# Reordering the SyncE queue of each chunk in an mLSTM cell followed by a squared-ReLU FFN

## Chip, cores, metric

The kernel runs on one core of a Trainium2 chip. The time is device microseconds of that core, the median of five runs. TensorE is called PE below, VectorE DVE, ScalarE ACT, GpSimd POOL, and SyncE SP; SP does no arithmetic here, it issues nearly all DMAs.

## The reference

Two stages. First an mLSTM cell for 4 batches x 8 heads, 768 steps, head size 40:

```python
m_new = np.maximum(f_gate[:, :, t] + m, i_gate[:, :, t])
f_stab = np.exp(f_gate[:, :, t] + m - m_new)
i_stab = np.exp(i_gate[:, :, t] - m_new)
C = f_stab * C + i_stab * outer(vt, kt);  n = f_stab * n + i_stab * kt
y[:, :, t] = sigmoid(o_gate) * (C @ qt) / max(abs(n @ qt), 1)
```

Then the heads of a step are laid side by side into x, 3072 tokens x 320, and an FFN follows:

```python
h = np.maximum(x @ w_in, 0.0)        # 320 -> 2048
return h * h @ w_out                 # 2048 -> 320
```

## The kernel before

**Tiling.** A chunk s is 128 steps of one batch with all eight heads: 24 chunks, six per batch. Inside a chunk the recurrence becomes masked attention: scores k·q, a decay matrix W made from the gates, values, and a state C that is carried from chunk to chunk. Two chunks make one FFN group g of 256 tokens; there are 12 groups. Both FFN products run as Strassen-like block products, which need sums of x (`sums_of_x`, on POOL), of the hidden layer (`sums`, L760, on DVE) and of the weights.

**The interleaving.** The order of every engine's instructions is written by hand. The main loop (`for n, (which, g, i) in enumerate(parts)`) works on chunk s = 6 + n//4, in four parts `at` = 0 to 3. From s = 8 on, an even chunk runs beside the second FFN product (`ffn2_fast`, PE line L765) and an odd one beside the first (`ffn1_open` and `ffn1_close`, PE lines L841 and L890; `fast` is true there). One even and one odd chunk make a period; attention ends with s = 23 and the FFN goes on alone.

**The round trips through DRAM.** Three things are turned around by writing rows to a DRAM buffer and reading them back in another order:

- `pair_up(s + 3)` (L305): four DRAM-to-DRAM copies of k and q of a later chunk. `load_squares(s + 2)` (L327) reads them back in four DMAs as 32 x 32 squares, and DVE turns those (`turn_kq`, L334).
- `store_num` (L580) writes the attention's numerator tn; `load_num` (L585) brings it back in four DMAs; DVE then normalises it into x_sb (`normalise_turned`, first instruction L597, last L606).
- `store_rows` (L632) writes x_sb; `load_rows` (L637) reads it back as squares in four DMAs into xT; DVE turns those (`turn_squares`, L644). `sums_of_x` and the first FFN product of the group then read xT.

**What else SP issues for a chunk.** `load_part(s + 4, 0)` and `(…, 2)` (L945) for k and v; `load_A(s + 2)` (L352), the gate sums; `load_o(s + 4)` (L342), the output gates; and the FFN's result rows (L801 and L806 in even chunks). SP works this list strictly in order: an instruction that waits holds up all behind it. The output gates get their sigmoid four chunks at a time, in part 3 of chunks 11, 15 and 19 (`sigmoid`, L345 on ACT); the last of the four is the chunk s + 4 that was asked for in part 1 of the same chunk.

**What stands behind those on DVE and ACT.** On DVE, in an even chunk: `turn_kq` (L334), `weighted` (L467), `ffn2_fast`'s first add (L781), tn (L568), `turn_squares` of the odd chunk before (L644), then `sums` (S4, L760), an add (L781), `scale_q` (L515), and further adds. On ACT after the sigmoid: the ReLU L907 and the copy L785, which PE's L765 of the next chunk needs. PE holds its PSUM banks until DVE's L908 to L911 have read them.

Of the kernel before, what the change touches and what calls it, by code (L numbers as in the profile page):

```python
# [29 lines left out]
def kernel(  # L30
# [259 lines left out]
    def load_parts(s):  # L290
        d = st.setdefault(s, {})
        kq, va = d["kq"], d["va"] = kq_b[s % NKQ], va_b[s % NKQ]
        return (kq[:, 0, :, :D], k), (kq[:, 1, :, :D], q), (va[:, :, :D], v)
# [4 lines left out]
    KQ_SQ, X_SQ = 7, 6  # L298
# [37 lines left out]
    def load_o(s):  # L336
        b, c = divmod(s, NB)
        r, (s0, s1) = next((r, (a, z)) for r, (a, z) in enumerate(RUNS) if a <= s < z)
        if s == s0:
            st["og", r] = ld.tile([P, 4, H, D], F32, name="og")  # L340
        og = st.setdefault(s, {})["og"] = st["og", r][:, s - s0]
        nc.sync.dma_start(og, o_gate[b, :, c * P : (c + 1) * P, :].rearrange("h p d -> p h d"))  # L342

    def sigmoid(s):
        nc.scalar.activation(st[s]["og"], st[s]["og"], AF.Sigmoid)  # L345
# [89 lines left out]
    def scores(s, o=(False, False)):  # L435
        d = st[s]

        sc = [bank(o[i]) for i in range(2)]
        d["sc"] = sc
        if s >= KQ_SQ:  # L440
            for j in range(PR):
                for keys in HALVES:
                    for i in range(2):
                        rows = slice(DP * i, DP * i + D)
                        nc.tensor.matmul(
                            sc[i][keys, j, :], lhsT=d["kT"][rows, j, keys], rhs=d["qT"][rows, j, :], start=(j == 0),
                            stop=True, skip_group_check=True,
                        )
            return
        for j in range(PR):  # L450
            for i in range(2):
                rows = slice(DP * i, DP * i + D)
                nc.tensor.matmul(
                    sc[i][:, j, :], lhsT=d["kT"][rows, j, :], rhs=d["qT"][rows, j, :], start=True, stop=True,
                )
# [279 lines left out]
    def sums_of_weights(i):  # L735
        if i < 3:
            T[i] = late.tile([P, NPAIR, DH], F32, name=f"T{i}", bufs=1)[:]
        if i == 0:
            nc.vector.tensor_tensor(T[0], B12, B11, op=ALU.subtract)
        elif i == 1:  # L740
            nc.vector.tensor_tensor(T[1], B22, T[0], op=ALU.subtract)
        elif i == 2:
            nc.vector.tensor_tensor(T[2], B21, T[1], op=ALU.subtract)
        else:

            nc.vector.tensor_tensor(B12, B22, B12, op=ALU.subtract)
# [99 lines left out]
    def ffn1_begin(g):  # L846
        new_g2(g)
        xT = st["xT", g]
        begun = st["begun"] = [
            (ps_h.tile([P, 4, P], F32, name="h_ps"), ffn.tile([P, 4, P], F32, name="r_sb", bufs=4)) for _ in range(2)  # L850
        ]
        for q, (X, m1) in enumerate(begun):
            blocks(X, F11, xT[:, 0, 0, :], q, True)
            nc.scalar.copy(m1[:], X[:])
        for q, (X, m1) in enumerate(begun):
            blocks(X, F12, xT[:, 0, 1, :], q, False)
# [21 lines left out]
    def ffn1_rows(g, q, first):  # L878
        xT, xs = st["xT", g], st["xs"]
        X, Y, V, Z = st["f1"]  # L880
        lo, hi = HALVES
        pairs = (
            ((X, lo, xT[lo, 0, 2, :], False), (Y, hi, xT[hi, 1, 2, :], first)),
            ((V, lo, xT[lo, 1, 2, :], first), (Z, hi, xs[hi, 1, :], False)),
        )
        for pair in pairs:
            for n in range(4):
                for cols in HALVES:
                    for to, rows, rhs, start in pair:
                        nc.tensor.matmul(  # L890
                            to[cols, n, :], lhsT=w_in2[rows, 4 * q + n, cols], rhs=rhs,
                            start=(start and n == 0), stop=True, skip_group_check=True,
                        )
# [29 lines left out]
    def do(f, s):  # L923
        if 0 <= s < NT:
            f(s)
# [16 lines left out]
    def load_part(s, i):  # L942
        b, c = divmod(s, NB)
        dst, src = load_parts(s)[i]
        nc.sync.dma_start(dst, src[b, :, c * P : (c + 1) * P, :].rearrange("h p d -> p h d"))  # L945
# [65 lines left out]
    for u in range(8):  # L1011
        s = 2 + u // 2
# [69 lines left out]
            parts += [(1, g + 2, i) for i in range(4)]  # L1082
    LAST = (17, 17, 18, 18, 18)
    assert LAST[-1] == len(pieces)
    for n, (which, g, i) in enumerate(parts):
        s, at = 6 + n // 4, n % 4
        if n == 5:
            brought.close()
            late = ctx.enter_context(tc.tile_pool(name="late", bufs=1, side="right"))
        even = s >= 8 and s % 2 == 0  # L1090
        fast = which == 1
        if at == 0:
            if s < 8 or even:
                do(scores, s)
            if even:
                do(turn_kq, s + 1)
            if s < 8 or even:
                do(weighted, s)
        if at == 1:
            if even:  # L1100
                do(lambda s: scores(s, ("h", "h")), s + 1)
            if fast:
                ffn1_rows(g, 0, True)
            do(attend_turned, s)
            do(decays, s + 1)
            do(mask, s + 1)
            if n > 4 and not even and not fast:
                do(turn_kq, s + 1)
            do(decay_C, s + 1)
            if s > X_SQ and not fast:  # L1110
                do(turn_squares, s - 1)
            do(store_num, s)
            if s > 6:
                do(lambda s: load_part(s, 0), s + 4)
                do(load_num, s)
                if not even:
                    do(load_squares, s + 2)
                do(load_A, s + 2)
                do(lambda s: load_part(s, 2), s + 4)
                if 8 <= s < 20:  # L1120
                    load_o(s + 4)
            else:
                do(load, s + 4)
                do(load_num, s)
            do(pair_up, s + 3)
        if 5 <= n < 8:
            sums_of_weights(n - 5)
        if n == 6:
            sums(1, slice(0, NPAIR), (1, 2))
        if n == 8:  # L1130
            sums_of_weights(3)
            sums(1, slice(0, NPAIR), (3,))
        if n == 9:
            sums(1, slice(0, NPAIR), (4,))
        if which == 2 and i == 3 and g == NG - 2:
            sums(g + 1, slice(0, NPAIR), (2,))
        if which == 2 and g > 1 and i < 2:
            sums(g, slice(0, NPAIR), (3 + i,))
        if n == 0:
            ffn1_begin(g)  # L1140
            sums_of_x(g)
            sums_of_win(2)
        if at == 3 and s >= 8 and s % 2 == 0 and s // 2 - 1 < NG:
            sums_of_x(s // 2 - 1)
        if at == 2 and not fast:
            if n > 4:
                do(scale_q, s + 1)
        if at == 3:
            if s % 4 == 3:
                for r in range(s + 1, min(s + 5, NT)):  # L1150
                    sigmoid(r)
        if fast:
            if i % 2:
                ffn1_close(g, i // 2, i == 1)
                if at == 1 and g > 2:
                    do(turn_kq, s + 1)
                    do(turn_squares, s - 1)
            else:
                ffn1_open(g, i // 2)
                if i == 0 and g > 2:  # L1160
                    sums(g - 1, slice(0, NPAIR), (2,))
            if at == 2 and g > 2:
                do(scale_q, s + 1)
        elif g == 0:
            ffn2(g, *divmod(i, 2))
        else:
            ffn2_fast(g, i)
        if at == 2:
            do(lambda s: weigh(s, masked=True), s + 1)
            ffn1_square()  # L1170
            if n < 4:
                do(turn_kq, s + 1)
                do(scale_q, s + 1)
            if even:
                do(weighted, s + 1)
            do(normalise_turned, s)
            do(store_rows, s)
            if s < 7 or even:
                do(load_squares, s + 2)
            do(load_rows, s)  # L1180
            if s < 7:
                do(load_A, s + 2)
        if at == 0:
            ffn1_square()
        if n < 5:
            while rounding.done < LAST[n]:
                rounding.step()
# [30 lines left out]
```

## Time and profile before

| | us |
|---|---|
| median of 5 runs | 510.88 (507.30 to 512.22) |
| profiled execution, its own time | 508.48 |
| span of the profiled execution | 506.7 |
| PE busy | 493.7 (97%) |
| weight loads busy | 457.1 (90%) |
| DVE busy | 350.4 (69%) |
| ACT busy | 249.6 (49%) |

The profiled execution has 1.8 us around its span and lies 2.4 us under the median. The granted TensorE clock was 1.00. PE's busy share is made of overlapping matmuls whose ends are modelled, so it is read together with the time that a period takes.

### The profile page before, as it was taken

Reading aid. Unit: us, or ns where it says so; the run is one execution under the profiler, and the core shown is the slowest. Engines: PE = TensorE matmul, PEld = TensorE weight load, DVE = VectorE, ACT = ScalarE, POOL = GpSimd, SP = SyncE. Lnnn points to the kernel's source line nnn. Section 1 sums busy time; section 2 is a strip of 40 time slices with the busy share of each in tenths; the row PEclk is TensorE's granted clock in tenths of the full one; section 3 lists DMA queues with packets and bytes.
Section 4 is the critical chain, followed back from the end, with each engine's and each line's share of the span. In section 5 each row is a group of like instructions: output and inputs, shape, how many; then the busy total and the mean of one; then the engine's idle time right before and its main releaser. Section 6 shows DMA issues by size and latency. Waiting matters only on the chain.

```text
span 506.7 us, 13829 instructions
## 1 busy us (share of the span) xinstructions
PE 493.7 (97%) x5640; PEld 457.1 (90%) x5641; DVE 350.4 (69%) x646; ACT 249.6 (49%) x492; POOL 118.4 (23%) x138
## 2 busy tenths in 40 slices
PE   9988999999999999999999989999999999999997
PEld 4867878897799999999999988999989999999997
DVE  8588968889956956847937738757658866635441
ACT  3767888853541650672641752551753550433400
POOL 3346743321232031013033014024005030020000
PEclk9999999999999999999999999999999999999999
DMA  9999899856747747748847757667656632210000
GB/s 190 226 215 209 249 211 188 192 100 141 157 116 162 146 108 159 159 115 164 164 103 159 149 122 166 127 153 162 117 144 143 124 91 51 71 25 15 1 27 26
DMA packets 238238, 67.74 MB, mean 134 GB/s; under 512 B 185600, under 2 KB 232704, under 8 KB 238176
## 3 DMA queue, kind: packets, MB, share of 16 engines
q1 hardware_dynamic: 238080, 66.68, 61.7%
q8 instruction: 44, 0.72, 0.6%
q10 hardware_dynamic: 96, 0.20, 0.1%
q14 instruction: 18, 0.15, 0.1%
HBM read 54.56 MB, written 17.86 MB: 143 GB/s over the span
## 4 chain that ended last, share of the span: by engine, by line
PE 72%; SPq 8%; DMA 8%; DVE 4%; ACT 3%; issue 3%; POOL 1%; DVEq 0%; POOLq 0%; ACTq 0%
PE h_ps L765 23%; PE h_ps L841 19%; PE h_ps L890 6%; PE h_ps L674 4%; PE h_ps L711 3%; PE numT L551 3%; SPq L327 2%; DMA og<-in_o_gate_dram 2%; DMA num_rows<-tn 2%; DMA xT<-x_rows 2%; SPq L305 2%; PE hp L490 2%; SPq L585 2%; DMA x_rows<-x_sb 2%; PE idle L934 1%
## 5 line engine op out<-in xcount | busy, mean ns | idle before, releaser
L377 POOL TENSOR_SCALAR_AFFINE_SELECT A_bc<-A_bc 128x1024 f32<-128x1024 f32 x22 | 24.6, 1118 | 139.2 <-ACT kq L387 123.6
L765 PE MATMUL h_ps<-T,S 128*128 128x160 f32 x352 | 51.5, 299 | 0.8 <-DVE g_c L909 0.8
L765 PEld LDWEIGHTS h_ps<-T,S 128*128 128x128 f32 x352 | 49.0, 190 | 1.0 <-PE h_ps L765 1.0
L765 PE MATMUL h_ps<-w_out,g 128*128 128x160 f32 x336 | 49.2, 303 | 0.4 <-ACT y_sb L785 0.4
L765 PEld LDWEIGHTS h_ps<-w_out,g 128*128 128x128 f32 x336 | 46.1, 190 | 1.9 <-issue 1.2
L401 ACT ACTIVATE A_bc<-A_bc,b_T 128x128 f32<-128x128 f32 x144 | 44.2, 391 | 6.7 <-POOL A_bc L377 6.4
L871 ACT COPY r_sb<-h_ps 128x512 f32<-128x512 f32 x18 | 10.6, 587 | 72.2 <-PE h_ps L841 72.2
L841 PE MATMUL h_ps<-xT,w_in 128*128 128x128 f32 x320 | 42.8, 278 | 0.0
L841 PE MATMUL h_ps<-lent_t,w_in 128*128 128x128 f32 x320 | 42.2, 275 | 0.0
L841 PEld LDWEIGHTS h_ps<-xT,w_in 128*128 128x128 f32 x320 | 38.9, 192 | 1.0 <-issue 0.7
L890 PE MATMUL h_ps<-xT,w_in 64*64 64x128 f32 x960 | 39.7, 273 | 0.0
L841 PE MATMUL h_ps<-lent_t 128*128 128x128 f32 x320 | 39.2, 276 | 0.1
L841 PEld LDWEIGHTS h_ps<-lent_t,w_in 128*128 128x128 f32 x320 | 38.9, 192 | 0.0
L841 PEld LDWEIGHTS h_ps<-lent_t 128*128 128x128 f32 x320 | 37.3, 192 | 0.5 <-POOL lent_t L836 0.3
L890 PEld LDWEIGHTS h_ps<-xT,w_in 64*64 64x64 f32 x960 | 34.8, 133 | 2.5
L781 DVE TENSOR_TENSOR y_sb<-y_sb,h_ps 128x160 f32<-128x160 f32 x44 | 14.0, 318 | 29.9 <-PE h_ps L765 29.8
L413 POOL TENSOR_TENSOR vw<-va,A_bc 128x328 f32<-128x328 f32 x15 | 13.6, 904 | 78.4 <-issue 45.9
L674 PE MATMUL h_ps<-xT,w_in 128*128 128x256 f32 x128 | 29.6, 383 | 1.2 <-POOL w_in L230 0.6
L568 DVE STREAM_TRANSPOSE tn<-numT 128x256 f32<-128x256 f32 x36 | 15.6, 446 | 22.0 <-PE numT L551 22.0
L765 PE MATMUL h_ps<-w_out,g_c 128*128 128x160 f32 x192 | 28.0, 302 | 1.4 <-ACT y_sb L785 1.4
L644 DVE STREAM_TRANSPOSE xT<-xT 128x384 f32<-128x384 f32 x18 | 10.1, 559 | 26.4 <-DMA xT<-x_rows 26.4
L765 PEld LDWEIGHTS h_ps<-w_out,g_c 128*128 128x128 f32 x192 | 26.3, 190 | 2.1 <-ACT y_sb L785 1.5
(188 smaller groups left out, 1082.0 us busy)
## 6 DMA issues: line engine op xcount, KB each, us to landing
A_bc<-a_rows SPq DMA_DIRECT2D x22, 512.0 KB, 4.8
num_rows<-tn SPq DMA_DIRECT2D x18, 256.0 KB, 2.4
kq<-num_rows SPq DMA_DIRECT2D x72, 64.0 KB, 2.0
raw<-in_moe_w_out_dram SPq DMA_DIRECT2D x7, 640.0 KB, 4.2
kqT<-kq_rows SPq DMA_DIRECT2D x34, 128.0 KB, 3.4
kq<-in_k_dram SPq DMA_DIRECT2D x24, 160.0 KB, 4.0
va<-in_v_dram SPq DMA_DIRECT2D x24, 160.0 KB, 5.0
og<-in_o_gate_dram SPq DMA_DIRECT2D x24, 160.0 KB, 4.8
```

The costliest lines, as they stand in the source:

```text
L377: nc.gpsimd.affine_select(A[:], A[:], compare_op=ALU.is_ge, fill=-1e30, base=0, pattern=[[0, H], [1, P]], channel_multiplier=-1,)
L401: nc.scalar.activation(d["W"][:, i * n + h, :], A[i][:, h, :], AF.Exp, bias=b_T[:, b, c, i * n + h : i * n + h + 1],)
L413: nc.gpsimd.tensor_tensor(d["vw"][:], d["va"][:], d["W"][:, :, P - 1 : P].to_broadcast([P, H, D1]), op=ALU.mult,)
L551: nc.tensor.matmul(numT[i][halves[g], e, :], lhsT=va_w[s % NKQ][:, h * D1 : h * D1 + DP], rhs=d["P"][h % 2][:, h // 2, :] if s < KQ_SQ els ...
L568: nc.vector.transpose(to[:, 2 * i : 2 * i + 2], numT[i][:, :2, :].rearrange("p c t -> p (c t)"))
L674: nc.tensor.matmul(hs[i][:, n, :], lhsT=w_in[:, a, fb * P : (fb + 1) * P], rhs=xT[:, :, a, :], start=(n == 0 and a == 0), stop=False,)
L711: nc.tensor.matmul(o_ps, lhsT=st["g2", g][:, fb, j * P : (j + 1) * P], rhs=w_out[:, fb, :], start=(fb == 0), stop=(fb == NF - 1),)
L765: nc.tensor.matmul(to, lhsT=lhsT[:, p], rhs=rhs[:, p, :], start=(start and p == 0), stop=(p == NPAIR - 1), skip_group_check=True,)
L781: add = lambda to, a, b: nc.vector.tensor_tensor(to, a, b, op=ALU.add)
L841: nc.tensor.matmul(to[:, n, :], lhsT=lhsT[:, 4 * q + n, :], rhs=rhs, start=(start and n == 0), stop=True, skip_group_check=True,)
L871: nc.scalar.copy(m1[:], X[:])
L890: nc.tensor.matmul(to[cols, n, :], lhsT=w_in2[rows, 4 * q + n, cols], rhs=rhs, start=(start and n == 0), stop=True, skip_group_check=True,)
```

## The change

Only the order of SP's list changes, and the place of one DVE instruction. No instruction is added or removed: SP has the same DMAs before and after, and so have the others.

SP's list for a chunk from s = 8 on, waits left out:

| | before | after |
|---|---|---|
| even s | num store, k, num load x4, A, v, gates, copies x4, L801, x store, squares x4, x load x4, L806 | num store, k, num load x4, squares x4, A, L801, x store, v, gates, x load x4, copies x4, L806 |
| odd s | num store, k, num load x4, squares x4, A, v, gates, copies x4, x store, x load x4 | num store, k, num load x4, squares x4, x store, A, v, gates, x load x4, copies x4 |

Chunk 7 is changed like an odd one (it has no gates; an FFN row store goes ahead of the x store). On DVE, in even chunks, `turn_squares` of the odd chunk before moves from part 1 to part 2: it now comes after S4 and the first add behind it, and ahead of `scale_q`.

```diff
+    def prefetch(s):
+        do(lambda s: load_part(s, 2), s + 4)
+        if 8 <= s < 20:
+            load_o(s + 4)
...
-            if s > X_SQ and not fast:
+            if s > X_SQ and not fast and not even:
                 do(turn_squares, s - 1)
             do(store_num, s)
             if s > 6:
                 do(lambda s: load_part(s, 0), s + 4)
                 do(load_num, s)
-                if not even:
-                    do(load_squares, s + 2)
-                do(load_A, s + 2)
-                do(lambda s: load_part(s, 2), s + 4)
-                if 8 <= s < 20:
-                    load_o(s + 4)
+                do(load_squares, s + 2)
+                if even:
+                    do(load_A, s + 2)
             else:
                 do(load, s + 4)
                 do(load_num, s)
-            do(pair_up, s + 3)
+                do(pair_up, s + 3)
...
         if at == 2 and not fast:
+            if even:
+                do(turn_squares, s - 1)
             if n > 4:
                 do(scale_q, s + 1)
...
             do(store_rows, s)
-            if s < 7 or even:
+            if s < 7:
                 do(load_squares, s + 2)
+            else:
+                if not even:
+                    do(load_A, s + 2)
+                prefetch(s)
             do(load_rows, s)
-            if s < 7:
+            if s > 6:
+                do(pair_up, s + 3)
+            else:
                 do(load_A, s + 2)
```

## The prediction

> **What bounds the kernel.** I read the windows view first, one row per period (odd chunk, then even chunk), cut where PE starts the odd chunk's first L841. Columns: stretch, its length, busy time of each engine.
>
> ```profile
> 154.96:192.53 37.57, 37.57 (x514) 36.55 (x513) 27.35 (x55) 16.88 (x34) 8.43 (x10) 1.00 0.67 144
> 229.83:268.74 38.91, 38.16 (x515) 36.70 (x514) 27.51 (x55) 16.88 (x34) 10.57 (x14) 1.00 0.68 142
> 268.74:308.81 40.07, 37.85 (x514) 36.51 (x513) 26.68 (x54) 21.06 (x40) 8.24 (x9) 1.00 0.66 142
> 345.95:385.20 39.25, 38.16 (x515) 36.68 (x514) 26.25 (x50) 21.13 (x40) 6.86 (x8) 1.00 0.63 134
> ```
>
> A period with the same matmuls takes 37.57 when nothing stops PE. Three take 1.3, 2.5 and 1.7 more; with 0.4 and 0.2 in two others, all stalls from chunk 8 on are about 6 us. That is all a new order can win. The Trainium skill (Perfetto Trace Analysis, "Identifying the Most-Contended Engine") says to judge headroom by weight-load busy share, not matmul busy: here 90%, so 10%, or 50 us. The stall-free row has weight loads at 36.55 of 37.57, so what a period can give back is the 6 us; I take the rows.
>
> Next, PE's rows in order of time, with the idle time ahead of each and its releaser:
>
> ```profile
> 218.86 1.35 PE L765 MATMUL h_ps<-w_out,g 128*128 128x160 f32 x8 [0.40 <-ACT y_sb L785]
> 266.40 2.44 PE L765 MATMUL h_ps<-w_out,S 128*128 128x160 f32 x16 [0.61 <-DVE y_sb L781]
> 296.72 3.53 PE L765 MATMUL h_ps<-w_out,g_c 128*128 128x160 f32 x24 [1.38 <-ACT y_sb L785]
> 306.53 2.44 PE L765 MATMUL h_ps<-w_out,S 128*128 128x160 f32 x16 [0.84 <-DVE y_sb L781]
> 368.46 1.73 PE L765 MATMUL h_ps<-T,S 128*128 128x160 f32 x11 [0.82 <-DVE g_c L909]
> 382.92 2.44 PE L765 MATMUL h_ps<-w_out,S 128*128 128x160 f32 x16 [0.27 <-DVE y_sb L781]
> ```
>
> So three kinds of stall. Behind L781 stands DVE's wait for xT, behind L785 ACT's wait for the last output gates; the list of waits has both:
>
> ```profile
> DVE xT L644 <- DMA xT<-x_rows: 26.4, 6, 5.8
> ACT og L345 <- DMA og<-in_o_gate_dram: 18.3, 3, 6.7
> ```
>
> Last, SP in order of time for odd chunk 15, then ACT's and DVE's waits that follow:
>
> ```profile
> 279.79 0.38 SPq L580 DMA_DIRECT2D num_rows<-tn  x1
> ...
> 287.83 0.82 SPq L352 DMA_DIRECT2D A_bc<-a_rows  x1
> 288.70 0.60 SPq L945 DMA_DIRECT2D va<-in_v_dram  x1
> 289.34 1.07 SPq L342 DMA_DIRECT2D og<-in_o_gate_dram  x1
> 290.46 2.69 SPq L305 DMA_DIRECT2D kq_rows<-in_k_dram  x2
> 293.20 1.98 SPq L305 DMA_DIRECT2D kq_rows<-in_q_dram  x2
> 295.27 0.53 SPq L632 DMA_DIRECT2D x_rows<-x_sb  x1
> 297.66 1.87 SPq L637 DMA_DIRECT2D xT<-x_rows  x4
> ```
> ```profile
> 295.53 0.47 ACT L345 ACTIVATE og<-og 128x320 f32<-128x320 f32 x1 [6.71 <-DMA og<-in_o_gate_dram]
> ```
> ```profile
> 303.57 0.58 DVE L644 STREAM_TRANSPOSE xT<-xT 128x384 f32<-128x384 f32 x1 [5.31 <-DMA xT<-x_rows]
> ```
>
> x_sb of chunk 15 was ready at 288.55 (end of DVE L606), but its store left at 295.27, behind A, v, gates and copies; DVE then stood 5.31 us. The gates left at 289.34 and landed at 295.5; ACT stood 6.71 us. Both waits end at PE.
>
> Below, "+t" is t us after the start of the current period (192.53, 229.83, 268.68, ...).
>
> **Odd x store ahead of A, v, gates, copies; xT turned later.** Without the four items ahead, the store leaves 6.7 us sooner, the rows land near +26, and L644, now behind the add of the even chunk's second product quarter, is due near +31.4 (PE ends that quarter at 186.0 in the period from 154.96, the add takes 0.3). The six waits (26.4 us of DVE) go. Only three reach PE: L781 gives 0.61, 0.84 and 0.27 on PE, 2.4 with the weight loads' share. Nothing is late in its place on DVE: S4 needs no xT. POOL's sums of x now start behind a later L644, but also behind `vw` and the mask, and end before PE's L841 as in the stall-free period. **-2.4.**
>
> **Even chunk's tail: num store of the odd chunk.** Even chunks lose squares from behind the x store and get v, gates and copies there. Before, the time from x store to the next num store was 6.8, 7.2, 6.9, 7.2, 6.7, 7.3, 7.5: squares 3.5, x load 2, L806 and gaps. After: the x store lands 2.35 later (L637's gap in odd chunks), v 0.6 and gates 1.0 fitting inside; x load 1.95; copies 3.75 (2.5 + 1.23); L806 0.6: 8.7, or 1.5 more. SP also waits with all this for x_sb, which DVE finishes at +1.3 (chunks 8 and 18) to +2.0 (chunk 10). In chunks 12 to 16 x_sb came at +2.0 to +3.0 because L644 held DVE; that delay goes. So the num store of the odd chunk leaves at +10.1 to +10.9; I take +10.5. Before: +8.1, +9.6, +10.5, +11.1, +10.4, +11.3, mean 10.2.
>
> From num store to L597 took 6.7, 5.8, 7.0, 5.9, 7.9 in chunks 11 to 19; with 6.7, L597 starts at +17.2. Its price: at chunk 19 it started at +19.2 and PE lost 1.0 (0.82 at L909 plus pipeline); at chunk 15, +18.0, nothing was lost. So DVE is in time, and chunk 19's stall becomes smaller.
>
> **Gates now behind the x store (chunks 11, 15, 19).** L597 to the end of L606 is 1.85: x_sb at +19.1, and the squares (num load from +13, 2.3 us, squares 3 us, so done by +18.3) cover most of the wait for it. Then the store 0.5, A 0.7, v 0.6: gates issued near +20.9. Before: +19.1, +20.7, +21.3. Landing takes 5.0 to 6.1 (the same three): +26.5. PE starts 1.2 after landing (217.64 to 218.86: sigmoid, ReLU, copy). Without a wait it starts at +25.9 in chunk 12 and +26.5 in 16 and 20 (0.55 of L542 more). Stalls: 1.8 + 1.2 + 1.2 = 4.2, against 0.4 + 1.4 + 1.0 (chunk 20's stands behind L909, and would stand here alone) = 2.8. **+1.4.** From both sides: landing at +25.0 makes it -2.8; at +28, +5.
>
> **At nothing.** Squares of even chunks leave 3 us or more sooner; the copies they read end 4 us ahead, where a copy lands 2.2 to 5.3 after issue, so SP may lose up to 1 us on the slow ones. Even A leaves 3 us later, lands near +2, and ACT's L387 may wait 1 us; ACT's next hard need is L907 at +8.9. Odd A leaves 2 us later, lands near +25.5, where L387 wants it at +25.7 (255.53): cover none, but the exponentials behind it end some 10 us before PE's L551. v is needed three chunks later. The copies behind the odd x load end 2 us sooner, because A, v and gates now fill SP's 2.3 us wait for the x store. Together 0, from -0.5 to +1.5.
>
> **Sum.** -2.4 + 1.4 + 0 = -1.0: 508.48 becomes 507.5; with the 2.4 between that execution and the median, 509.9; rounded, 510.0.
>
> **A rule against the change.** In one period, 182.67 to 221.65, SP's slices sum to 32.6 of 39.0 us. The Trainium skill (Perfetto Trace Analysis, "DMA Optimizations") says that when descriptor generation is the bottleneck, visible as an issuing engine full of slices, the DMAs should be balanced over several issuing engines. By that, order alone moves nothing: 510.9. By the rows PE waits for two particular transfers, not for SP's total, and order moves those: 509.9. No run here shows DMAs spread over more engines in this loop.
>
> **Rivals.** *Head of line, slower.* All that SP puts behind the even x store hangs on x_sb. If the tail is 10.2 instead of 8.7 (copies stretching to 4.8 as in odd chunks 11 and 15, x_sb at +2.4), the num store leaves at +12 and L597 at +18.7, past the +18.2 from which L909 and `weighted` reach PE. Chunks 10 to 20 then lose about 0.5 each, 3 in all, and gates land 1.5 later in three chunks, 4.5: -1.0 + 7.5 = +6.5, 517.4. For it: chunk 19 shows the price, and slack is only 1 us. Against: x_sb comes sooner once L644 doesn't wait.
>
> *Both stalls go, faster.* If x_sb comes at +1.3 and the tail takes 7.1 as before, the num store leaves near +8.6, gates land by +25, and -2.4 - 2.8 = -5.2: 505.7. For it: chunk 9 had +8.1. Against: the tail holds two transfers more.
>
> *Nothing reaches PE:* the gates take exactly what xT gives, 510.9.
>
> **Numbers.** The likeliest case with the last one (507.5 to 514) 0.62; head of line 0.25 (514 to 520); both stalls gone 0.13 (504.5 to 507). Some 1% is what a measurement of this kernel can tell from no change: under 505.8 or over 516.0. Half or a little more of the fast case lies below: faster 0.08. Of the slow case most, 0.20, and 0.02 of unforeseen waits lie above: slower 0.22; same 0.70. Range 505.8 to 517.5, leaving out the ends of both.
>
> **What would show it.** Right: L644's wait gone or under 3 us in all; no PE stall behind L781 in L765's S products; L345's wait 20 us or more; num stores near +10.5; periods of 229.83 and 268.74 near 37.9 and 39. Wrong: L597 after +18.2 in most periods with PE waiting at L909 or L551, or gates issued before +19.5.

## The result: 0.6% slower

The changed kernel takes 512.5 us in the median of 27 runs (509.1 to 516.0), the kernel before 509.9 in the same series (48 runs): ratio 1.0059, 95% interval 1.0041 to 1.0077. By the ratio that is 3.0 us; the two medians differ by 2.6. The forecast was 510.0, a gain of 0.2%; the time lies inside its range. Its sign was wrong, and the difference is under the 1% that the prediction took as measurable: with this many runs half a per cent can be told.

The changed kernel's profiled execution took 510.85, with a span of 509.1 (before: 508.48 and 506.7). The windows view, cut into periods as before, columns as there, the granted clock ahead of the last two:

```profile
194.20:232.90 38.70, 36.90 (x482) 35.68 (x481) 24.59 (x47) 19.77 (x38) 4.66 (x7) 1.00 0.68 145
270.70:308.29 37.59, 37.59 (x514) 36.56 (x513) 26.19 (x51) 21.13 (x40) 7.71 (x9) 1.00 0.72 155
345.12:387.78 42.66, 39.61 (x514) 38.30 (x513) 26.68 (x53) 21.13 (x40) 6.68 (x10) 0.96 0.67 145
```

The third period of the prediction's table (40.07) is now free of stalls (37.59), and the one from 229.83 went from 38.91 to 37.80. But the period of chunks 19 and 20 went from 39.25 to 42.66, and that of chunks 11 and 12 to 38.70; it takes 36.82 without a stall, and before it took:

```profile
192.53:229.83 37.30, 36.90 (x483) 35.68 (x481) 24.55 (x47) 19.76 (x38) 4.43 (x6) 1.00 0.67 142
```

PE's rows in order of time, with the idle time ahead of each and its releaser in brackets, show where PE stands idle in those two:

```profile
221.93 4.61 PE L765 MATMUL h_ps<-w_out,g 128*128 128x160 f32 x32 [1.80 <-ACT y_sb L785]
367.38 2.41 PE L765 MATMUL h_ps<-T,S 128*128 128x160 f32 x16 [0.57 <-DVE g_c L909]
375.15 6.27 PE L765 MATMUL h_ps<-w_out,g 128*128 128x160 f32 x32 [2.48 <-ACT y_sb L785]
```

No row is left behind L781. Both large stalls are those of the output gates, and the list of waits (us in total, times, longest) has no line of DVE's L644 any more, while ACT's wait grew from 18.3 to:

```profile
ACT og L345 <- DMA og<-in_o_gate_dram: 20.8, 3, 8.7
```

The same 32 matmuls took 4.61 us behind the first stall and 6.27 behind the second. Two windows show why, one over the second stall and one right behind it; the first number behind each length is PE's busy time, the third from the end the granted clock:

```profile
371.74:375.15 3.41, 0.93 (x28) 0.81 (x24) 0.16 (x2) 1.19 (x4) 0.00 (x0) 1.00 0.47 70
375.15:378.57 3.42, 3.42 (x13) 3.42 (x14) 2.75 (x6) 3.42 (x5) 0.00 (x0) 0.50 0.55 173
```

After the 2.48 us stand PE ran at half clock until 378.57: another 1.66 us. How that stall came about is read from SP's rows in order of time, from the even chunk 18's A to the odd chunk 19's gates:

```profile
344.82 0.60 SPq L352 DMA_DIRECT2D A_bc<-a_rows  x1
...
346.50 0.38 SPq L632 DMA_DIRECT2D x_rows<-x_sb  x1
346.93 0.61 SPq L945 DMA_DIRECT2D va<-in_v_dram  x1
347.60 1.17 SPq L342 DMA_DIRECT2D og<-in_o_gate_dram  x1
350.76 3.11 SPq L637 DMA_DIRECT2D xT<-x_rows  x4
...
357.12 0.38 SPq L580 DMA_DIRECT2D num_rows<-tn  x1
...
366.06 0.38 SPq L632 DMA_DIRECT2D x_rows<-x_sb  x1
...
367.75 0.70 SPq L342 DMA_DIRECT2D og<-in_o_gate_dram  x1
```

The even chunk's tail, the time from its x store to the next num store, took 10.62 here. 4.21 of it was the x store's own landing, for which the x load waits; in the five even chunks before, it took 2.1 to 2.7. A left 1.68 ahead of the x store here, and 2.9 to 4.7 ahead in those. So the odd num store left at +12.0, L597 started at +18.9 (364.07), x_sb was there at +20.9, and only then could the x store and, behind it, A, v and the gates go: issued at +22.6, landed at +28.8.

In this pair of executions the seven periods add up to 0.7 us more. The other 1.7 of the span lie ahead of chunk 9 (its period starts at 156.63 instead of 154.96), where the clock was at half from 41 to 47 us. Twelve of the fourteen profiled executions here, one of the unchanged kernel among them, show such a stretch somewhere between 32 and 74 us; the profile of before on which the prediction stands has none, which fits its lying 2.4 us under the median. So one pair of profiles can't weigh 3 us; the runs of the parts below do.

### The profile page after: what moved, and what is told of

Its sections match the earlier page's. It is cut to its first block, busy times and chain, and to the rows that moved or that the text cites. A ratio compares the mean times of both kernels' runs of the same rounds, so it can differ in the third digit from the quotient of the medians.

```text
span 509.1 us, 13827 instructions
## 1 busy us (share of the span) xinstructions
PE 497.9 (98%) x5640; PEld 462.0 (91%) x5641; DVE 352.3 (69%) x646; ACT 250.0 (49%) x492; POOL 118.1 (23%) x138
## 4 chain that ended last, share of the span: by engine, by line
PE 88%; DMA 5%; DVE 4%; ACT 1%; SPq 1%; issue 1%; DVEq 0%
PE h_ps L765 32%; PE h_ps L841 23%; PE h_ps L890 7%; PE h_ps L674 4%; PE h_ps L711 3%; PE numT L551 3%; DMA og<-in_o_gate_dram 2%; PE hp L490 2%; PE idle L934 1%; PE tp L453 1%; PE h_ps L685 1%; PE numT L542 1%; PE tp L445 1%; PE h_ps L445 1%; DMA kq<-num_rows 1%; PE tp L430 1%
## 5 line engine op out<-in xcount | busy, mean ns | idle before, releaser
L377 POOL TENSOR_SCALAR_AFFINE_SELECT A_bc<-A_bc 128x1024 f32<-128x1024 f32 x22 | 25.1, 1141 | 152.8 <-ACT kq L387 143.2
L765 PE MATMUL h_ps<-w_out,g 128*128 128x160 f32 x336 | 50.8, 309 | 4.3 <-ACT y_sb L785 4.3
L765 PEld LDWEIGHTS h_ps<-w_out,g 128*128 128x128 f32 x336 | 47.7, 195 | 5.9 <-ACT y_sb L785 4.5
L781 DVE TENSOR_TENSOR y_sb<-y_sb,h_ps 128x160 f32<-128x160 f32 x44 | 14.0, 319 | 46.8 <-PE h_ps L765 46.8
L871 ACT COPY r_sb<-h_ps 128x512 f32<-128x512 f32 x18 | 10.6, 587 | 71.3 <-PE h_ps L841 71.3
L841 PE MATMUL h_ps<-xT,w_in 128*128 128x128 f32 x320 | 42.8, 278 | 0.0
L841 PE MATMUL h_ps<-lent_t,w_in 128*128 128x128 f32 x320 | 42.2, 275 | 0.0
L841 PEld LDWEIGHTS h_ps<-xT,w_in 128*128 128x128 f32 x320 | 38.9, 192 | 1.1 <-issue 0.7
L841 PE MATMUL h_ps<-lent_t 128*128 128x128 f32 x320 | 39.1, 275 | 0.0
L841 PEld LDWEIGHTS h_ps<-lent_t,w_in 128*128 128x128 f32 x320 | 38.9, 192 | 0.0
L841 PEld LDWEIGHTS h_ps<-lent_t 128*128 128x128 f32 x320 | 37.3, 192 | 0.2 <-POOL lent_t L836 0.2
L674 PEld LDWEIGHTS h_ps<-xT,w_in 128*128 128x128 f32 x128 | 24.4, 196 | 4.3 <-ACT xT L653 0.8
L908 DVE TENSOR_TENSOR r_sb<-r_sb,h_ps 128x512 f32<-128x512 f32 x20 | 13.7, 686 | 20.8 <-PE h_ps L841 14.3
```

The lines of the kernel that those rows point to most:

```text
L377: nc.gpsimd.affine_select(A[:], A[:], compare_op=ALU.is_ge, fill=-1e30, base=0, pattern=[[0, H], [1, P]], channel_multiplier=-1,)
L674: nc.tensor.matmul(hs[i][:, n, :], lhsT=w_in[:, a, fb * P : (fb + 1) * P], rhs=xT[:, :, a, :], start=(n == 0 and a == 0), stop=False,)
L765: nc.tensor.matmul(to, lhsT=lhsT[:, p], rhs=rhs[:, p, :], start=(start and p == 0), stop=(p == NPAIR - 1), skip_group_check=True,)
L781: add = lambda to, a, b: nc.vector.tensor_tensor(to, a, b, op=ALU.add)
L841: nc.tensor.matmul(to[:, n, :], lhsT=lhsT[:, 4 * q + n, :], rhs=rhs, start=(start and n == 0), stop=True, skip_group_check=True,)
L908: tt(U2[:], U2[:], Y[:], op=ALU.add)
```

## The experiments

All ratios are to the kernel before on the same chip, with 95% intervals. All kernels compute everything. The first question was which part of the change costs. The expectations set three answers against each other: theory G (the gates land too late and PE stands for them), theory or rival E (the even chunk's tail makes all of SP's list late, the head of the line), and rival C (the clock varies by itself).

### The kernel before, unchanged

> The kernel before once more, unchanged, for the clock of each of its runs. Theory G (gates: the output gates land later, ACT and with it PE stand longer, and a long stand of PE is followed by microseconds at half clock): mean granted clock 0.995 or more in most runs, against 0.989 to 0.993 in most runs of the changed kernel. Rival C (the clock varies by itself from run to run): the same spread as the changed kernel, 0.989 to 0.997. Time ratio to before 1.000 under both.

Measured: 1.0013 [0.9990, 1.0036]. So the change's 1.0059 is not chance. The mean granted clock of its runs was 0.993 (0.989 to 1.000), that of the changed kernel's 0.992 (0.989 to 0.997): the 0.995 that theory G expected did not come, and a run's mean clock does not tell the two kernels apart. Its profile had periods of 38.75, 38.38, 39.64, 38.63 and 39.38 behind the first, that is 8.6 us of stalls, against 6.5 in the profile of before (37.57 and 36.82 taken as free of stalls). What the stalls sum to varies by 2 us from one execution to the next.

### One part at a time

Odd chunks alone in the new order, even chunks and the turn of x as before:

```diff
+                new = not even
-                if not even:
+                if new or not even:
                     do(load_squares, s + 2)
-                do(load_A, s + 2)
...
+                if even or not new:
+                    do(load_A, s + 2)
+                if not new:
+                    prefetch(s)
...
-            do(pair_up, s + 3)
+            if s < 7 or not (not even):
+                do(pair_up, s + 3)
...
             do(store_rows, s)
+            new = s > 6 and (not even)
+            if new and not even:
+                do(load_A, s + 2)
+            if new:
+                prefetch(s)
...
             do(load_rows, s)
+            if new:
+                do(pair_up, s + 3)
```

> The new order in odd chunks alone (x store ahead of A, v, gates; copies last); even chunks and the place of xT's turning as before. Theory G (the gates behind the x store of odd chunks are the whole loss): xT's waits gone, gates near +19.5 to +21, PE stalls behind L785 of 1 to 2 us in three chunks: ratio to before 0.998 to 1.004. Theory G plus E (the even chunk's tail adds to it by a later num store): num stores at +8 to +10, gates sooner, ratio 0.992 to 0.997.

Measured: 0.9940 [0.9915, 0.9965], as theories G and E together expected. L644's waits are gone but for one of 0.7, with the turn at its old place. Odd num stores left at +8.4 to +10.3, gates at +19.1 to +20.4; the last gates landed at +25.8, +25.1 and +27.0, and two stalls behind L785 remain, 1.08 and 1.53.

Even chunks alone in the new order, odd chunks and the turn as before; the diff is to the kernel with the odd part alone:

```diff
-                new = not even
+                new = even
...
-            if s < 7 or not (not even):
+            if s < 7 or not (even):
                 do(pair_up, s + 3)
...
-            new = s > 6 and (not even)
+            new = s > 6 and (even)
```

> The new order in even chunks alone; odd chunks and the place of xT's turning as before. Theory G: nothing gained, nothing lost, ratio 0.998 to 1.003. Theory E: odd num stores 1 to 1.5 us later, and with them gates and the odd x store, xT's waits longer: ratio 1.004 to 1.012.

Measured: 1.0069 [1.0048, 1.0089], as theory E expected. Odd num stores left at +11.5 to +11.9 in chunks 11 to 17 (before: +9.6, +10.5, +11.1, +10.4), so x, still last in odd chunks, left at +26.7 to +27.5. This loss comes by way of x, not of the gates, behind which PE stood 0.51 at most. DVE's wait for x then reached 8.46 us, and PE's S products behind it waited and ran at half clock (4.12 instead of 2.44). DVE's and PE's rows in order of time:

```profile
349.16 0.58 DVE L644 STREAM_TRANSPOSE xT<-xT 128x384 f32<-128x384 f32 x1 [8.46 <-DMA xT<-x_rows]
```
```profile
352.08 4.12 PE L765 MATMUL h_ps<-w_out,S 128*128 128x160 f32 x16 [3.61 <-DVE y_sb L781]
```

The later turn of x alone, on the kernel before:

```diff
-            if s > X_SQ and not fast:
+            if s > X_SQ and not fast and not even:
                 do(turn_squares, s - 1)
...
         if at == 2 and not fast:
+            if even:
+                do(turn_squares, s - 1)
```

> Only the turning of odd xT moved behind S4 and the add, SP's order as before. xT lands near +31 to +34 and DVE now asks for it at +31.4, so its wait shrinks from 26 us to some 8 and S4 no longer stands behind it: PE stalls behind L781 mostly gone, gates' stalls unchanged, ratio 0.994 to 0.998. If xT's transfer itself is what PE needs (through the sums of x on POOL), ratio 1.000.

Measured: 1.0008 [0.9987, 1.0029], not the 0.994 to 0.998 that was expected first. L644's waits fell from 26.4 to 8.4 us, 2.2 at most, and nothing was won: in chunks 13 to 19 num stores came at +12.0 to +13.0, L597 at +19.3 to +20.6, and PE stood at L909's product quarter (1.25 at most), at L445 and at L841 instead.

So the odd part gives -0.6%, the even part +0.7%, the turn nothing that can be measured. On top of the odd part, even part and turn together cost 1.2%, more than the 0.7% of the even part by itself; the difference is only just clear of the intervals.

### Gates or head of line

The changed kernel with the odd chunks' gates ahead of the x store:

```diff
     def prefetch(s):
         do(lambda s: load_part(s, 2), s + 4)
-        if 8 <= s < 20:
+        if 8 <= s < 20 and s % 2 == 0:
             load_o(s + 4)
...
                 do(load_squares, s + 2)
                 if even:
                     do(load_A, s + 2)
+                elif 8 <= s < 20:
+                    load_o(s + 4)
```

> The changed kernel, but in odd chunks the output gates leave right behind the squares, ahead of the x store. Theory G: gates issued near +18 of the period instead of +19.3 to +22.6, landing by +24.5; PE's stalls at L765 behind L785 (1.8 and 2.5 us) fall under 0.5 each; ratio to before 0.992 to 0.996. Rival E (what costs is the even chunk's tail: the next num store leaves later): L909's stall of 0.6 and chunk 19's num store at +12 stay, ratio stays at 1.003 to 1.006.

Measured: 0.9890 [0.9857, 0.9923], 504.0 us: one DMA, moved three places ahead in the odd chunks' list, turns the loss into a gain of 1.1%. All periods but one are free of stalls (37.57 or 36.82); the exception, chunk 19's, takes 38.91. SP's rows of that worst chunk and ACT's row:

```profile
363.16 1.06 SPq L342 DMA_DIRECT2D og<-in_o_gate_dram  x1
364.82 0.38 SPq L632 DMA_DIRECT2D x_rows<-x_sb  x1
```
```profile
366.83 0.47 ACT L345 ACTIVATE og<-og 128x320 f32<-128x320 f32 x1 [3.27 <-DMA og<-in_o_gate_dram]
```

The gates leave while SP would wait for x_sb, and the x store behind them leaves up to 1.6 us after x_sb, which costs PE nothing. In the other two chunks ACT waits 0.67 and 0.66. Here they land 3.2 to 3.7 us after their issue, in the changed kernel 5.3 to 6.2.

The same place of the gates without the even part and without the later turn; the diff is to the kernel with the odd part alone:

```diff
-        if 8 <= s < 20:
+        if 8 <= s < 20 and s % 2 == 0:
             load_o(s + 4)
...
                 if new or not even:
                     do(load_squares, s + 2)
+                if not even and 8 <= s < 20:
+                    load_o(s + 4)
```

> As the odd chunks alone, with the odd chunks' gates right behind the squares, ahead of the x store; even chunks as before. Theory G: equal to the changed kernel with gates ahead, ratio 0.987 to 0.991. Theory G plus E: better than that by 1 to 3 us, ratio 0.983 to 0.987. If the even chunk's new order has a gain of its own (squares sooner), worse: 0.991 to 0.995.

Measured: 0.9899 [0.9863, 0.9936]. Every period is free of stalls. So with the gates ahead the even part and the turn neither cost nor give anything that can be measured (both intervals are about 0.35% to either side); what they cost in the changed kernel, they cost by way of the gates.

The opposite: the changed kernel with the odd chunks' gates behind the copies.

```diff
-        if 8 <= s < 20:
+        if 8 <= s < 20 and s % 2 == 0:
             load_o(s + 4)
...
             if s > 6:
                 do(pair_up, s + 3)
+                if 8 <= s < 20 and not even:
+                    load_o(s + 4)
```

> The changed kernel with the odd chunks' gates as the last of SP's list, behind the copies: gates near +26 to +28, landing +31 to +33. Theory G: PE stands 5 to 7 us behind L785 in chunks 12, 16 and 20; with the clock at half for some 3.4 us after each stand (1.7 us lost each): ratio to before 1.035 to 1.05 and a mean clock of 0.98 to 0.985. Without the clock's part: 1.025 to 1.035 and a clock of 0.992.

Measured: 1.0352 [1.0318, 1.0387], at the lower end of what was expected with the clock's part. The gates landed at +32.0, +32.3 and +33.5, 5.5, 7.0 and 4.7 later than in the changed kernel. PE's three stands became 7.26, 6.41 and 7.32, and each was followed by half clock: the 32 matmuls behind them took 6.64, 7.24 and 7.35, against 4.61. The span is 20.8 longer, 16.7 of it the stands.

### Is the gates' wait the cost by itself?

The changed kernel with the sigmoids regrouped so that ACT waits for no gate: chunk 11 takes three instead of four, and the later groups begin with the chunk itself, in part 1 of chunks 15, 19 and 23.

```diff
+            if s % 4 == 3 and s > 11:
+                for r in range(s, min(s + 4, NT)):
+                    sigmoid(r)
...
-            if s % 4 == 3:
-                for r in range(s + 1, min(s + 5, NT)):
+            if s in (7, 11):
+                for r in range(s + 1, s + 5 if s == 7 else s + 4):
                     sigmoid(r)
```

> The changed kernel, with the sigmoids of the gates regrouped so that ACT never takes one whose gates were asked for in the same chunk: after chunk 11 only those of 12 to 14, in chunk 15 those of 15 to 18, in chunk 19 of 19 to 22, in chunk 23 of 23 (there in the second quarter, where ACT stands). Two table loads more. Theory G: ACT's wait for gates gone, no PE stall behind L785, ratio to before 0.988 to 0.993. Rival E: ratio 1.002 to 1.006, as the changed kernel. Rival C: the clock's mean stays at 0.99.

Measured: 0.9960 [0.9939, 0.9982], between the two expectations. ACT's wait and the stalls behind L785 are gone, and with them 1.0% of the changed kernel's time, so the gates' wait is what made it slower. But it stays 0.7% behind the version with the gates ahead. Num stores left at +10.2 to +12.6, and in chunks 15 and 19 L597 started at +19.4 and +19.6. DVE's row and PE's row of chunk 15:

```profile
288.70 0.17 DVE L597 TENSOR_SCALAR dm<-kq 128x8 f32<-128x8 f32 x1 [3.90 <-DMA kq<-num_rows]
```
```profile
294.51 1.11 PE L445 MATMUL h_ps<-kqT 40*64 40x128 f32 x29 [1.34 <-issue]
```

After L597 DVE finishes x, empties PE's banks and turns k and q, without a pause until 294.42 but for 0.28 us; PE's scores, which read the turned k and q, start at 294.51 (a stand of 1.34, and of 1.41 in chunk 19). The row names no releaser; DVE's rows do. This is the head-of-line stall of the prediction's rival. In the changed kernel L597 of chunk 15 started at +15.8. That PE's stand for the gates in chunk 12 had given SP's list that time is likely, but was not tested.

The same regrouping on the kernel before:

> The kernel before with the same regrouped sigmoids. Theory G: its stalls behind L785 (0.4 and 1.4 us) go, those behind L781 stay, ratio 0.994 to 0.998. Rival E: 1.000. If xT's waits were the larger cost, this stays clearly slower than the changed kernel with early sigmoids, by 2 us or more.

Measured: 1.0004 [0.9984, 1.0024], where theory G expected 0.994 to 0.998. The gates' wait of 18.3 us is gone and nothing was won: stalls behind L781 (1.57, 0.57, 0.57) and at L445 (0.18, 0.37, 0.59) took its place.

### The kernel before with one DMA moved

```diff
                 if not even:
                     do(load_squares, s + 2)
+                if not even and 8 <= s < 20:
+                    load_o(s + 4)
                 do(load_A, s + 2)
                 do(lambda s: load_part(s, 2), s + 4)
-                if 8 <= s < 20:
+                if even and 8 <= s < 20:
                     load_o(s + 4)
```

> The kernel before, with the gates of odd chunks right behind the squares, ahead of A and v. If its own gates' waits cost it what the trace shows (0.4, 1.4 and part of 1.0 us), ratio 0.994 to 0.997. If xT's waits take their place, as with the early sigmoids, 0.999 to 1.001.

Measured: 0.9923 [0.9885, 0.9960]. ACT's wait fell to 3.0, 3.1 and 4.0, and the gates landed 3.3 to 4.1 after issue. L644 still waits up to 6.74, with 1.54 behind L781 on PE in chunk 16. This is more than was expected and does not agree with the regrouped sigmoids, which took that wait away altogether and won nothing. There are only 7 runs, and the profiled execution does not show the gain: its seven periods take 268.5, against 268.0 before. So the size of this gain stays open.

### Issuing from a second engine

The kernel before with v and gates issued by ACT's queue from chunk 11 and 12 on:

```diff
-        nc.sync.dma_start(og, o_gate[...])
+        eng = nc.scalar if s > 11 else nc.sync
+        eng.dma_start(og, o_gate[...])
...
-        nc.sync.dma_start(dst, src[...])
+        eng = nc.scalar if i == 2 and s > 10 else nc.sync
+        eng.dma_start(dst, src[...])
```

> The kernel before, with v and gates of the chunks from 11 or 12 on issued from ACT's queue in place of SP's, in the same places of the program. If SP's total of issue time is short (the rule on balancing issuing engines), num stores, gates and odd x stores come 1.5 to 3 us sooner and the ratio is 0.988 to 0.994. If only the order of single transfers counts: gates sooner, the odd x store 1.6 us sooner, xT's waits shorter by as much: 0.994 to 0.998. If ACT's own list is held up by the issues: 1.000 or more.

Measured: 0.9981 [0.9959, 1.0004]. SP has 25 DMAs fewer, and stalls behind L781 and L785 are gone. But the odd num stores leave at +11.2 to +12.3, L597 starts as late as +20.3, and PE stands at L445 (2.29 at most). SP's own list of waits shows that it was not freed (the lines of this kernel count one higher; L638 is the x load):

```profile
SPq L638 <- DMA va<-in_v_dram: 17.6, 6, 3.8
```

SP's x load waits for the landing of v, which ACT issued, and five of the even chunks' num stores wait for it too (12.3 us, 3.2 at most). In the trace the transfers share landing semaphores: an x load at 205.47 waits for semaphore 104, which v's landing had set at 205.45. The even tail grew to 9.8 to 10.8, from 6.7 to 7.3 before. The Trainium skill's rule that the prediction weighed (Perfetto Trace Analysis, "DMA Optimizations") says that balancing may help where descriptor generation is the bottleneck. Here the total of SP's list fell and the time hardly moved; but since SP still waited for the DMAs that it no longer issued, this run does not test a second queue that is free of the first.

### A short tail

The changed kernel, where even chunks have v, gates and copies ahead of L801 and the x store, so that only the x load and L806 stand between x store and num store:

```diff
                 if even:
                     do(load_A, s + 2)
+                    prefetch(s)
+                    do(pair_up, s + 3)
...
                 if not even:
                     do(load_A, s + 2)
-                prefetch(s)
+                    prefetch(s)
             do(load_rows, s)
-            if s > 6:
+            if s > 6 and not even:
                 do(pair_up, s + 3)
-            else:
+            elif s < 7:
                 do(load_A, s + 2)
```

> The changed kernel with v, gates and copies of even chunks back ahead of L801 and the x store, where SP otherwise stands for x_sb; squares stay ahead, odd chunks stay as changed (gates behind the x store). Tail from x store to next num store 5 to 6 us, num stores near +7.5 to +8.5. If the tail is what makes the gates late: gates near +18, no PE stall behind L785, ratio 0.988 to 0.991. If the gates' place behind the odd x store alone does it: as the odd chunks alone, 0.993 to 0.997.

Measured: 1.0138 [1.0099, 1.0176], slower than any expectation. The tail did shorten, to 4.6 to 6.6 in chunks 10 to 18. SP's rows of chunk 16:

```profile
316.76 0.62 SPq L342 DMA_DIRECT2D og<-in_o_gate_dram  x1
...
322.37 0.38 SPq L632 DMA_DIRECT2D x_rows<-x_sb  x1
325.94 1.86 SPq L637 DMA_DIRECT2D xT<-x_rows  x4
```

x_sb was ready at 319.82, 2.55 before its store left (5.46 and 7.52 in chunks 10 and 14), and then SP stood 3.2 us for the store to land, with nothing left to issue meanwhile. Odd num stores came at +10.6 to +14.5, gates landed at +28.0, +30.7 and +30.8, and the stalls were of several kinds (3.01, 1.48 and 1.75 behind L785, 1.86 and 2.28 at L841). The tail as the prediction counted it, from x store to num store, isn't the quantity that matters. The time from x_sb's end to the num store is: it grew (8.6 to 12.6 in chunks 10 to 18, against 8.2 to 10.8 in the changed kernel), because the store left late and the landing wait behind it was left empty. The changed kernel's order is better than this one.

## Why the prediction was wrong, by its own steps

The step that failed is the price of the gates, the +1.4. It is a sum of three stalls with nothing for the clock behind them, and the even chunk's A, which stands right ahead of the x store where the longest of the three began, was put at nothing after a look at ACT alone. In this pair of profiles the half clock is the whole miss: the seven periods were forecast 1.0 shorter and came out 0.7 longer, and 1.66 of that 1.7 is half clock. Over all runs the miss is larger, 4 us, and the versions that keep the gates from being late win 5 us (regrouped sigmoids) and 8.6 us (gates ahead) over the changed kernel.

**What can be won.** About 6 us of stalls; right. Without any stall in the seven periods, the run with odd order and gates ahead is 1.0% or 5.2 us faster.

**xT's waits.** They went, and no stall behind L781 is left, as said. But the -2.4 priced them as if PE's stall ended with its wait. On the kernel before, taking away the gates' wait by the regrouped sigmoids, or most of xT's by the later turn, gave nothing (1.0004 and 1.0008): the next late thing took its place. The one run that speaks against this is the kernel before with its gates ahead (0.9923).

**The tail.** Right on the mean: forecast 8.7, measured in chunks 10 to 18 9.03, 8.12, 8.45, 8.14, 10.62, mean 8.9. Odd num stores: forecast +10.5, measured +10.3, +10.8, +9.7, +10.4, +12.0. L597: forecast +17.2, mean +17.1. What the mean hides is chunk 18. Chunk 19's stall behind L909 fell from 0.82 to 0.57.

**The gates.** Issue: forecast +20.9, measured in chunks 11, 15 and 19 +21.2, +19.3 and +22.6. Landing: forecast +26.5, measured +26.5, +25.4, +28.8. The sum of stalls, 4.2, was met too, but by luck: 1.80, none and 2.48 in place of 1.8, 1.2 and 1.2. What failed is that this sum stood for three chunks near their mean, at a constant price:

- Lateness isn't spread evenly. Chunk 16 lands early enough, chunk 20 over 2 us too late, and behind that stand the clock was halved: 1.66 us here, in no term of the sum. With it, the period of chunk 19 takes 3.4 longer than before, and the other six together gave only 2.7.
- Two parts of the sum were off in the same direction. By the prediction's numbers the odd part with its old tail was its "both stalls gone", -5.2, and the longer tail took +4.2 of it. Measured: -3.1 (0.6% of 510) for the odd part, since with the short tail too the gates land at +25.1 to +27.0, not by +25; and +6.1 for even part and turn, each to about 1.5 us. The tail was right in its mean length; its price by way of the gates was too low.

**At nothing.** The squares, A, v and copies: no stall of PE in the changed kernel stands behind them. But v and A aren't free for what follows. Right behind A and v the gates that ACT waits for landed 4.3 to 6.6 us after their issue (once 3.8); right behind squares or copies, in four kernels, 3.0 to 4.1. The prediction took the long landing as the gates' own, so it looked for earlier issue only. The even chunks of the changed kernel point to A: there the gates leave right behind v, with A 2.8 us or more ahead, and landed 3.3 to 4.4 after issue. So does the x store: in the kernels where SP issues everything, each of the fifteen that left less than 2 us behind an A took 3.5 to 4.7 to land. Chunk 18's was one of them (4.21), and its 2 us more came out at chunk 19's gates. No run moved A by itself.

**The signs.** L644's wait gone, no stall behind L781, L345's wait over 20 us (20.8), num stores near +10.5, and the period of 229.83 at 37.8: as stated, on a kernel that became slower. The period of 268.74 came out at 37.6, not near 39, since chunk 16's gate stall stayed away; and of the signs of being wrong, gates issued before +19.5, one chunk of three had it (+19.3). The signs tested the mechanism's parts, and none of them tested the price of the gates.

**The rivals.** Head of line, with its tail of 10.2 and num store at +12, is what chunk 19 did; the other chunks did not. Its price was to lie at L909 and `weighted` as well as at the gates; in the changed kernel nearly all of it came by the gates. Its second half (PE standing for DVE behind a late L597) shows in the version with regrouped sigmoids (1.34 and 1.41), and smaller with the later turn alone (0.68 and 0.54 at L445).

**What stays open.** The full 3.0 us is not closed from one pair of profiles: their periods differ by 0.7, and stalls vary from execution to execution. The mean granted clock over all runs, 0.992 for the changed kernel and 0.994 for the kernel before (on other chips, in the later series), would make about 0.9 us. That the rest are gate stalls follows from the versions with the gates ahead and with the regrouped sigmoids (1.7% and 1.0% faster than the changed kernel), not from a sum.

## What to carry to other kernels

In an in-order issuing queue, place each transfer by the slack of the one who waits for it, and count for every transfer that is moved back what is now issued right ahead of it, since that lengthens its landing as well as delaying its start. A stall that ends last may hide another close behind it, so test a removal by itself before giving it a price. And price a stall by its longest instance and by what the clock does after it, not by the mean.

## What the runs showed of the hardware

- After PE stood still for 2.48, 3.01, 3.61, 6.41, 7.26 and 7.32 us the granted clock was 0.50; after stands of 1.80, 1.75, 1.56 and 1.54 it stayed at 1.00. In between, the length of the stand does not decide: 1.86 was followed by half clock, 2.28 (both in the short-tail kernel) and 2.29 (second issuing engine) were not. What decides can be read from when the clock changed. Every stretch at half clock is 3.41 us long, or 6.83, or 10.24, but for a last one at the end of each trace; in one trace all changes lie on one grid of 3.41 us (in the changed kernel from 47.48 to 375.15, 96 steps). So I count PE's idle time in each step of that grid. Of all steps between 150 and 430 us that ran at full clock, in fourteen traces, the seven with 1.86 us idle or more were followed by a step at half clock, and none of the others, with 1.75 or less. The short-tail kernel's steps with the stands of 1.86 and 2.28:

```profile
289.30:292.71 3.41, 1.55 (x14) 1.38 (x13) 2.44 (x4) 3.39 (x5) 0.57 (x1) 1.00 0.59 148
367.81:371.22 3.41, 1.94 (x18) 1.74 (x16) 0.65 (x2) 3.41 (x8) 0.74 (x1) 1.00 0.69 173
```

  The first is idle for 1.86, and the next step ran at 0.50. The second holds only 1.47 of its stand, the rest falls into the next step, and the clock stayed at 1.00. The grid lies differently against the kernel's start in each trace, so where a stand falls on it is chance, and so is part of what the stand costs. The Trainium skill (TensorE: Matmul & The Clock Gate, Part 1) halves the clock after an idle window of about 3.4 us and says that the window runs freely. The grid agrees with such a window; but it need not be idle throughout, 1.86 of 3.41 us were enough here.
- A DMA of 160 KB (the gates that ACT waits for) landed 3.0 to 4.1 us after its issue behind smaller ones, or 4.3 to 6.6 (once 3.8) right behind one of 512 KB (A) and one of 160 KB (v) on the same queue. One of 192 KB (the x store) took 3.5 to 4.7 when it left less than 2 us behind A, and 2.1 to 2.7 in the changed kernel's even chunks with A further ahead.
- Moving v and gates to a second issuing queue took 25 DMAs off SP and changed the time by 0.2%, not distinguishable from none; SP still waited 17.6 and 12.3 us for the landing of v. Moving one DMA within SP's queue changed the time by 1.7%.
